# Head mix ahead of the softmax: one float32 matmul becomes three float32r matmuls of split operands

## The chip, the cores and the metric

The kernel runs on one core of one Trainium2 chip. The metric is the device time of one execution in microseconds, given as the median of several runs of the same program. The core's engines are TensorE (PE; its weight loads are shown as PEld), VectorE (DVE), ScalarE (ACT), GpSimd (POOL) and SyncE (SP), which issues nearly all DMA transfers. Each engine works through its own instructions in the order in which the program gives them; semaphores make one engine wait for another.

## The reference, cut to what matters

```python
# batch 2, 12 heads, 448 rows, head size 64
scores = scale * np.matmul(q, k.transpose(0, 1, 3, 2))
scores = np.einsum('bhij,hg->bgij', scores, w_pre)      # head mix ahead of the softmax
scores = scores - np.max(scores, axis=-1, keepdims=True)
attn = np.exp(scores)
attn = attn / (np.sum(attn, axis=-1, keepdims=True) + 1e-09)
attn = np.einsum('bhij,hg->bgij', attn, w_post)         # head mix behind it
attn_out = np.matmul(attn, v)
# rows (b, i) of 12 * 64 values go through two feed-forward layers, 768 -> 2048 -> 768 each
```

All inputs and outputs are float32. The change concerns the first `einsum`.

## The kernel before, in words

**Tiles, groups, steps.** The 448 query rows of each of the two batches are cut into four tiles of 120, 120, 120 and 88 rows. A tile is cut into groups of 10 rows, 12 groups for a tile of 120 and 9 for the tile of 88, so that there are NG = 90 groups. A group holds 10 rows times 12 heads = 120 partitions (GP), with the 448 keys along the free dimension. A loop over steps `s_` runs from -PL to NG + LAG, and in step s the work of several groups is in flight.

**One group's way.** For every head of a tile, `qk` (L193) computes 448 columns of scores in two float32r matmuls, and ScalarE copies them from PSUM into the tile's score buffer S (L600). `pull` (L205) lets SP issue a DMA that gathers one group's rows from S into a buffer "pull" of 120 x 448. `premix` (L221) multiplies the group by the block-diagonal `wpre` (120 x 120), one float32 matmul of 448 columns (L225, two records on TensorE), and VectorE takes the negated maximum of each row (L227). `exp` (L230) is ScalarE's exponential with the row sum as a by-product. `norm` (L213) adds 1e-9 to the sum, inverts it and scales the post-mix weights by it, three VectorE instructions (L216, L217, L219). `post` (L240) is the second mix, eight float32 matmul records per group, LAG = 3 steps behind the first; ScalarE copies its result (L258). When a tile is complete, `av` (L273) multiplies by v, six head pairs per tile.

**Order of the work.** In step s: pull of group s + PL, loads, premix of s, scores of one or two heads of the next tile, exponential of s, copies of these scores, query and key splits, normalisation of s - 1, second mix of s - 3, and whatever the table `also` or `av_at` holds for the step. This order is written out by hand; each engine follows it for its own instructions. The two PSUM buffers "mx" let the mix of group s + 2 start once the exponential of s has read its own.

**Lead times.** PL = 4 steps lie between a pull and its mix, and six buffers "pull" exist. Queries are loaded by SP six steps ahead and split by GpSimd (`split_q`, L165: a rounded copy and a subtraction) two steps ahead. The keys of the second batch are split head by head (`split_k`, L150: a VectorE cast and a GpSimd subtraction) while the last tile of the first batch gets its scores. The v loads of the first batch are issued in steps 0 to 3. `av_at` places three pairs two steps after the second mix of a tile ends, and three pairs half a tile later.

**Towards the feed-forward layers.** Three weight blocks are converted early, in steps that are counted from the third tile from the end (`conv_magnitude` on ScalarE, `conv_shift` and `conv_sign` on VectorE, `conv_round` on GpSimd). From step X on, which is PL steps before the last tile, no scores are left; ScalarE and GpSimd split the attention's results there (`split_x`, L440: a cast on ScalarE, L442, and a subtraction on GpSimd), and `conv_hi` and `conv_lo` split the converted weights. The layers' own matmuls (L447) are three float32r matmuls of split operands: high by high, high by low, low by high.

Of the kernel before, what the change touches and what calls it, by code (L numbers as in the profile page):

```python
# [7 lines left out]
F32 = mybir.dt.float32  # L8
R = mybir.dt.float32r
# [4 lines left out]
ALU = mybir.AluOpType  # L14
# [1 line left out]
PSUM = bass.MemoryType.PSUM  # L16

LAG = 3
PL = 4
EB = 384  # L20

W_MIN = 2.0 ** -15
# [13 lines left out]
def kernel(  # L36
# [15 lines left out]
    nc = tc.nc  # L52
    _, D, H, S = k.shape
# [6 lines left out]
    GP = G * H  # L60
# [3 lines left out]
    tiles = []  # L64
    groups = []
    for b in range(B):
        for i0 in range(0, S, GP):
            n = min(GP, S - i0)
            t = len(tiles)
# [7 lines left out]
    NTILE, NG = len(tiles), len(groups)  # L77
# [23 lines left out]
    with tc.manual_schedule():  # L101
# [30 lines left out]
        def load_v(b, c):  # L132
            t = late.tile([JP, HC, NJ, D], F32, tag=f"v{c}", bufs=1, name=f"v{c}")
            nc.sync.dma_start(out=t, in_=v[b, :, HC * c:HC * (c + 1)])
            v_t[b, c] = t
# [68 lines left out]

        def pull(g):  # L205
            ti, o, st, xn = groups[g]
            t = late.tile([GP, S], F32, tag="pull", bufs=PL + 2, name="pull")
            src = S_t[ti][bass.ds(o, xn, step=st)] if st > 1 else S_t[ti][o:o + xn]
            nc.sync.dma_start(t[:xn * H], src)  # L209
            d_t[g] = t  # L210


        def norm(g):  # L213
# [4 lines left out]
            wr = wr_t[g] = late.tile([GP, GP], F32, tag="wr", bufs=LAG + 1, name="wr")  # L218
            nc.vector.tensor_scalar(wr[:pm], wpost[:pm], sm, None, ALU.mult)  # L219

        def premix(g):  # L221
            pn = groups[g][3] * H
            d = d_t.pop(g)
            m = psA.tile([GP, 512], F32, tag="mx", bufs=2, name="mx")
            nc.tensor.matmul(m[:pn, :S], wpre[:pn, :pn], d[:pn], start=True, stop=True)  # L225
            nm = late.tile([GP, 1], F32, tag="nm", name="nm")
            nc.vector.tensor_reduce(nm[:pn], m[:pn, :S], axis=AX.X, op=ALU.max, negate=True)  # L227
            mx_t[g] = (m, nm)
# [79 lines left out]
        }  # L308
        for ti in range(NTILE - 1):
            lo = tiles[ti]["s"] + tiles[ti]["ng"] + LAG  # L310
            for z in range(2):
                av_at[lo + 2 + z * (tiles[ti + 1]["ng"] // 2)] = [(ti, 3 * z + a) for a in range(3)]


        P = {}
# [56 lines left out]
        def conv_hi(i):  # L372
            if i < len(blocks):
                hi = P["w"].tile([128, WC], R, tag="whi", bufs=3, name="whi")
                nc.scalar.copy(hi, b_t[i])  # L375
                w_t[i] = [hi]

        def conv_lo(i):
            if i < len(blocks):
                lo = P["w"].tile([128, WC], R, tag="wlo", bufs=3, name="wlo")  # L380
                nc.gpsimd.tensor_tensor(lo, b_t.pop(i), w_t[i][0].bitcast(F32), ALU.subtract)  # L381
                m = KD if blocks[i][0] == "in" else 2
                w_t[i] = [x.rearrange("p (k f) -> p k f", k=m) for x in (w_t[i][0], lo)]
# [56 lines left out]
        def split_x(kk, c, a, z, src, eng):  # L440
            h, l = x_pair(kk, c)
            nc.scalar.copy(h[:, a:z], src)  # L442
            eng.tensor_tensor(l[:, a:z], src, h[:, a:z].bitcast(F32), ALU.subtract)
# [82 lines left out]
            nc.sync.dma_start(out=wmix[nm], in_=src)  # L526
        load_q(1, 0)
        wpre = wmix["pre"]

        wpost = late.tile([GP, GP], F32, tag="wpost", bufs=1, name="wpost")  # L530
        for j in range(H // 2):
# [6 lines left out]
        nc.gpsimd.tensor_copy(  # L538
            wpost.rearrange("p (g x) -> p x g", g=H), wmix["post"].rearrange("p (x g) -> p x g", g=H)
        )  # L540
        for s_ in range(-PL, 6 - PL):
            for (ti, h) in qk_at.get(s_, []):
                if h % HC == 0 and h:
                    load_q(ti, h // HC)

        X = tiles[-1]["s"] - PL
        also = {}

        def at(s_, *fs):
            also.setdefault(s_, []).extend(fs)  # L550

        a = tiles[-3]["s"]
        for i in range(NC):
            at(a, lambda i=i: load_w(i))
            for z, f in enumerate((conv_magnitude, conv_shift, conv_sign, conv_round)):
                at(a + 3 + z, lambda f=f, i=i: f(i))
            a += 7
        at(X, open_early)
        at(X + 1, lambda: nc.sync.dma_start(out=alpha_sb, in_=alpha.rearrange("(k p) -> p k", p=128)))
        for kk in range(KD):  # L560
            at(X + 1 + kk, lambda kk=kk: split_x(kk, 0, 0, S, xT[:, kk, :S], nc.gpsimd))
        for i in range(NC):
            at(X + 2 + 3 * i, lambda i=i: conv_hi(i), lambda i=i: conv_lo(i))
        at(X + 7, lambda: load_w(3), lambda: load_w(4))
        at(NG, lambda: conv_a(3))
        at(NG + 1, lambda: conv_round(3))
# [5 lines left out]

        gs = {}
        for s_ in range(-PL, NG + LAG):
            for g in range(PL) if s_ == -PL else [s_ + PL] if 0 <= s_ < NG - PL else []:
                pull(g)
            for c in range(2) if s_ in k_first else ():
                load_k(k_first[s_], c)
            for ti in range(tps, NTILE, tps):
                if s_ == tiles[ti]["s"] + tiles[ti]["ng"] + LAG:  # L580
                    for c in range(4):
                        load_v(tiles[ti]["b"], c)
            if 0 <= s_ < 4:
                load_v(0, s_)
            if s_ in range(NG):
                premix(s_)
            kk = s_ - (NG - KD)
            if kk == 0:
                p0 = ptile()[:, :S]
            if 0 <= kk < KD:  # L590
                in_part(p0, 0, x_t, 0, kk, kk + 1)
            heads = qk_at.get(s_, [])
            pend = [
                qk0(ti, h) if s_ < 0 and h >= HC else qk(ti, h, s_ < 0 and h % 2)
                for (ti, h) in heads
            ]
            if s_ in range(NG):
                exp(s_)
            for d, p in pend:
                nc.scalar.copy(d, p)  # L600
            for (ti, h) in qk_at.get(s_ + 6, []):
                if h % HC == 0:
                    load_q(ti, h // HC)
            for (ti, h) in qk_at.get(s_ + 2, []):
                if h % HC == 0:
                    split_q(ti, h // HC)
            for (ti, h) in qk_at.get(s_ - 2, []):
                if ti % tps == tps - 1 and ti + 1 < NTILE:
                    split_k(tiles[ti + 1]["b"], h)
                    if h in (2, 5):  # L610
                        load_k(tiles[ti + 1]["b"], h // HC + 2)
            if s_ - 1 in range(NG):
                norm(s_ - 1)
            if s_ - LAG in range(NG):
                post(s_ - LAG)
                post_evac(s_ - LAG)
            if s_ == NG:
                p1 = in_chain(1, x_t, 0)
                gs[0, 0] = g_tile(0, 0)
                run(act1(p0, gs[0, 0], 0))  # L620
            if s_ == NG + 1:
                p2 = ptile()[:, :S]
                in_part(p2, 2, x_t, 0, 0, KD // 2)
            if s_ == NG + 2:
                in_part(p2, 2, x_t, 0, KD // 2, KD)
                gs[1, 0] = g_tile(1, 0)
                run(act1(p1, gs[1, 0], 1))
            for (ti, h) in av_at.get(s_, []):
                av(ti, h)
            for f in also.get(s_, []):  # L630
                f()
# [146 lines left out]
```

## Time and profile before

| | us |
|---|---|
| median of three runs | 704.34 |
| lowest and highest | 703.92 and 704.57 |
| the profiled execution, its own time | 703.76 |
| its span, first to last instruction | 701.9 |

| engine | busy us | share of the span | instructions |
|---|---|---|---|
| PE | 692.3 | 99% | 4164 |
| PEld | 608.9 | 87% | 4164 |
| DVE | 440.6 | 63% | 778 |
| ACT | 372.9 | 53% | 692 |
| POOL | 322.6 | 46% | 222 |

A matmul is pipelined, and its end is modelled, so that a busy PE is not yet PE at its peak; how far apart the starts of matmuls lie tells more than the duration listed for one. The chain that ended last is followed back from the last instruction, at each step to what released it or to the instruction before it on its engine. In the table of stretches the engines stand in the order PE, PEld, DVE, ACT, POOL, then come the granted clock (1.00 is full), the busy share of the DMA engines and GB/s. In a row of the timeline the bracket at the end holds the idle time of the engine just before the instruction and what ended it. The attention fills about the first 250 us, the two layers the rest.

### The profile page before, as it was taken

The numbers are of one execution on the slowest core, as the hardware profiler recorded it, in microseconds if no ns is written. First come the engines' busy times: TensorE is split into PE (matmuls) and PEld (weight loads), VectorE is DVE, ScalarE is ACT, GpSimd is POOL, SyncE is SP. The second block draws the span as 40 slices with busy tenths as digits, with TensorE's granted clock in tenths as the row PEclk, the third lists the DMA queues.
The fourth block names the chain that finished last, engine by engine and source line by source line (L and its number), as shares of the span: only waits on it lengthen the run. The fifth ranks groups of instructions, "written<-read, shape, count | busy, mean of one in ns | idle before, by whom it ended". The sixth has DMA issues, their size and how long they took to land.

```text
span 701.9 us, 11158 instructions
## 1 busy us (share of the span) xinstructions
PE 692.3 (99%) x4164; PEld 608.9 (87%) x4164; DVE 440.6 (63%) x778; ACT 372.9 (53%) x692; POOL 322.6 (46%) x222
## 2 busy tenths in 40 slices
PE   7999999999999999999999999999999999999998
PEld 3678778877787999999999999999999999999997
DVE  5565865456666458888874454358999999435311
ACT  5686566667776556656554443343444454445300
POOL 6231552112225335554567555544455455775630
PEclk9999999999999999999999999999999999999999
DMA  4855554346445022423334323322223323445302
GB/s 154 239 175 169 170 138 113 109 161 199 149 99 157 2 90 91 136 90 117 109 115 153 134 93 114 112 91 90 91 91 119 107 91 94 154 156 179 125 1 78
DMA packets 31874, 85.20 MB, mean 121 GB/s; under 512 B 5966, under 2 KB 21966, under 8 KB 31822
## 3 DMA queue, kind: packets, MB, share of 16 engines
q1 hardware_dynamic: 31678, 84.28, 37.2%
q8 instruction: 33, 0.54, 0.3%
q10 hardware_dynamic: 144, 0.23, 0.1%
q14 instruction: 19, 0.16, 0.1%
HBM read 62.47 MB, written 2.75 MB: 93 GB/s over the span
## 4 chain that ended last, share of the span: by engine, by line
PE 88%; POOL 4%; issue 3%; DMA 3%; ACT 1%; SPq 0%; DVE 0%; POOLq 0%; ACTq 0%
PE p L447 58%; PE pt L245 10%; PE mx L225 9%; PE av L282 6%; PE sc L198 4%; POOL wb L370 2%; DMA pull<-S 2%; POOL wlo L381 2%; PE sc L187 1%; DMA qst<-in_q_dram 1%; SPq L209 0%; ACT S L533 0%; ACT S L600 0%; POOL qT L170 0%; DVE o L697 0%
## 5 line engine op out<-in xcount | busy, mean ns | idle before, releaser
L381 POOL TENSOR_TENSOR wlo<-wb,whi 128x768 fp32r<-128x768 f32 x64 | 126.8, 1982 | 126.8 <-ACT whi L375 126.8
L370 POOL TENSOR_TENSOR wb<-wb,wst 128x768 int32<-128x768 int32 x64 | 125.6, 1962 | 102.1 <-DVE wb L363 78.1
L447 PE MATMUL p<-xh,whi 128*128 128x448 f32 x384 | 141.7, 369 | 0.0
L447 PE MATMUL p<-gl,whi 128*128 128x448 f32 x384 | 139.4, 363 | 0.0
L447 PE MATMUL p<-xl,whi 128*128 128x448 f32 x384 | 139.4, 363 | 0.0
L447 PE MATMUL p<-gh,whi 128*128 128x448 f32 x384 | 139.1, 362 | 0.0
L447 PE MATMUL p<-gh,wlo 128*128 128x448 f32 x384 | 138.4, 360 | 0.1
L447 PE MATMUL p<-xh,wlo 128*128 128x448 f32 x384 | 138.3, 360 | 0.0
L355 DVE TENSOR_SCALAR wb<-wb 128x768 f32<-128x768 f32 x64 | 53.1, 829 | 81.2 <-ACT wb L347 81.1
L347 ACT ACTIVATE wb<-wst 128x768 f32<-128x768 f32 x64 | 57.8, 904 | 68.9 <-DMA wst<-in_w_out_dram 48.1
L245 PEld LDWEIGHTS pt<-wr,e 120*112 120x112 f32 x720 | 86.8, 176 | 7.6 <-issue 2.3
L235 ACT ACTIVATE e<-mx,nm 120x448 f32<-120x448 f32 (+1 forms) x90 | 57.4, 638 | 59.9 <-DVE sm L216 46.8
L245 PE MATMUL pt<-wr,e 120*112 120x120 f32 x720 | 88.6, 266 | 0.0
L225 PE MATMUL mx<-pull,wmix_pre 120*120 120x448 f32 x180 | 84.0, 549 | 1.4 <-ACT e L235 1.0
L227 DVE TENSOR_REDUCE nm<-mx 120x1 f32<-120x448 f32 (+1 forms) x90 | 56.0, 622 | 44.4 <-PE mx L225 44.1
L375 ACT CAST whi<-wb 128x768 fp32r<-128x768 f32 x64 | 53.3, 832 | 50.6 <-PE p L447 32.4
L447 PEld LDWEIGHTS p<-xh,whi 128*128 128x128 f32 x384 | 72.1, 188 | 6.7 <-issue 1.2
L447 PEld LDWEIGHTS p<-gh,whi 128*128 128x128 f32 x384 | 72.1, 188 | 5.5
L447 PEld LDWEIGHTS p<-gh,wlo 128*128 128x128 f32 x384 | 71.8, 187 | 5.5 <-POOL wlo L381 0.5
L447 PEld LDWEIGHTS p<-xl,whi 128*128 128x128 f32 x384 | 72.1, 188 | 4.9 <-issue 0.9
L447 PEld LDWEIGHTS p<-xh,wlo 128*128 128x128 f32 x384 | 71.8, 187 | 5.0
L447 PEld LDWEIGHTS p<-gl,whi 128*128 128x128 f32 x384 | 72.1, 188 | 3.9
(52 smaller groups left out, 898.0 us busy)
## 6 DMA issues: line engine op xcount, KB each, us to landing
wst<-in_w_in_dram SPq DMA_DIRECT2D x32, 768.0 KB
wst<-in_w_out_dram SPq DMA_DIRECT2D x32, 768.0 KB
pull<-S SPq DMA_DIRECT2D x88, 210.0 KB
qst<-in_q_dram SPq DMA_DIRECT2D x20, 180.0 KB
kst<-in_k_dram SPq DMA_DIRECT2D x5, 672.0 KB
v<-in_v_dram SPq DMA_DIRECT2D x8, 336.0 KB
out_dram<-o SPq DMA_DIRECT2D x12, 224.0 KB
qst<-in_q_dram SPq DMA_DIRECT2D x8, 132.0 KB
```

The lines of the kernel that those rows point to most:

```text
L198: nc.tensor.matmul(p[:n, :S], t[:, o, a:a + n], kT[h], start=(o == 0), stop=(o == 1))
L225: nc.tensor.matmul(m[:pn, :S], wpre[:pn, :pn], d[:pn], start=True, stop=True)
L227: nc.vector.tensor_reduce(nm[:pn], m[:pn, :S], axis=AX.X, op=ALU.max, negate=True)
L235: nc.scalar.activation(out=e[:pn], in_=m[:pn, :S], func=ACTF.Exp, bias=nm[:pn], accum_out=sm[:pn])
L245: nc.tensor.matmul(p[:, c * GP:(c + 1) * GP], e[:pn, c * JP:(c + 1) * JP], wr[:pn], start=True, stop=True,)
L282: nc.tensor.matmul(p[64 * o:64 * o + 64, a % 3, :n], v_t[T["b"], h // HC][:, h % HC, c, :], MT[ti][:, c, h, :n], start=(c == 0), stop=(c = ...
L347: nc.scalar.activation(t, s[:, :, 1].bitcast(F32), ACTF.Abs)
L355: nc.vector.tensor_scalar(t, t, W_MAX, W_MIN, ALU.min, ALU.max)
L370: nc.gpsimd.tensor_tensor(n, n, st_t.pop(i)[:, :, 0].bitcast(I32), ALU.add)
L375: nc.scalar.copy(hi, b_t[i])
L381: nc.gpsimd.tensor_tensor(lo, b_t.pop(i), w_t[i][0].bitcast(F32), ALU.subtract)
L447: nc.tensor.matmul(p, wt[a], xt[c], start=(first and z == 0), stop=(last and z == 2))
```

## The change

For groups from RAW = 2 on, the mix ahead of the softmax is computed like the layers' matmuls: `wpre` is split once by GpSimd into a rounded high part and the rest, each group's pulled rows are split two steps ahead of their mix into a rounded copy `sh` and the rest (written back over the pulled rows by VectorE), and `premix` issues high by high, high by low, low by high as three float32r matmuls. The copy is ScalarE's for groups in `by_scalar` (two of three, with a few exchanged near the weight conversions) and VectorE's for the others. Groups 0 and 1 keep the float32 matmul. With it go: PL from 4 to 5 with still six pull buffers, queries loaded seven and split three steps ahead, `norm` moved in front of the split, the scores and the query and key splits of its step, all six pairs of `av` in one step, the v loads of the first batch in steps 9 to 12 and those of the second spread over four steps, and other steps for `split_x`, `conv_hi` and `conv_lo`.

```diff
@@ -16,7 +16,8 @@
 PSUM = bass.MemoryType.PSUM
 
 LAG = 3
-PL = 4
+PL = 5
+RAW = 2
 EB = 384
 
 W_MIN = 2.0 ** -15
@@ -204,7 +205,7 @@
 
         def pull(g):
             ti, o, st, xn = groups[g]
-            t = late.tile([GP, S], F32, tag="pull", bufs=PL + 2, name="pull")
+            t = late.tile([GP, S], F32, tag="pull", bufs=PL + 1, name="pull")
             src = S_t[ti][bass.ds(o, xn, step=st)] if st > 1 else S_t[ti][o:o + xn]
             nc.sync.dma_start(t[:xn * H], src)
             d_t[g] = t
@@ -218,11 +219,27 @@
             wr = wr_t[g] = late.tile([GP, GP], F32, tag="wr", bufs=LAG + 1, name="wr")
             nc.vector.tensor_scalar(wr[:pm], wpost[:pm], sm, None, ALU.mult)
 
+        def split_s(g):
+            if RAW <= g < NG:
+                pn = groups[g][3] * H
+                d = d_t.pop(g)
+                t = late.tile([GP, S], R, tag="sh", bufs=2, name="sh")
+                (nc.scalar.copy if g in by_scalar else nc.vector.tensor_copy)(t[:pn], d[:pn])
+                r = d.bitcast(R)
+                nc.vector.tensor_tensor(r[:pn], d[:pn], t[:pn].bitcast(F32), ALU.subtract)
+                d_t[g] = (t, r)
+
         def premix(g):
             pn = groups[g][3] * H
             d = d_t.pop(g)
             m = psA.tile([GP, 512], F32, tag="mx", bufs=2, name="mx")
-            nc.tensor.matmul(m[:pn, :S], wpre[:pn, :pn], d[:pn], start=True, stop=True)
+            if g < RAW:
+                nc.tensor.matmul(m[:pn, :S], wpre[:pn, :pn], d[:pn], start=True, stop=True)
+            else:
+                for z, (a, x) in enumerate(((0, 0), (0, 1), (1, 0))):
+                    nc.tensor.matmul(
+                        m[:pn, :S], wpre_r[a][:pn, :pn], d[x][:pn], start=(z == 0), stop=(z == 2)
+                    )
             nm = late.tile([GP, 1], F32, tag="nm", name="nm")
             nc.vector.tensor_reduce(nm[:pn], m[:pn, :S], axis=AX.X, op=ALU.max, negate=True)
             mx_t[g] = (m, nm)
@@ -308,8 +325,7 @@
         }
         for ti in range(NTILE - 1):
             lo = tiles[ti]["s"] + tiles[ti]["ng"] + LAG
-            for z in range(2):
-                av_at[lo + 2 + z * (tiles[ti + 1]["ng"] // 2)] = [(ti, 3 * z + a) for a in range(3)]
+            av_at[lo + 2] = [(ti, a) for a in range(H // 2)]
 
 
         P = {}
@@ -526,6 +542,7 @@
             nc.sync.dma_start(out=wmix[nm], in_=src)
         load_q(1, 0)
         wpre = wmix["pre"]
+        wpre_r = [late.tile([GP, GP], R, tag=f"wpre{z}", bufs=1, name=f"wpre{z}") for z in "hl"]
 
         wpost = late.tile([GP, GP], F32, tag="wpost", bufs=1, name="wpost")
         for j in range(H // 2):
@@ -538,13 +555,16 @@
         nc.gpsimd.tensor_copy(
             wpost.rearrange("p (g x) -> p x g", g=H), wmix["post"].rearrange("p (x g) -> p x g", g=H)
         )
-        for s_ in range(-PL, 6 - PL):
+        nc.gpsimd.tensor_scalar(wpre_r[0], wpre, 1.0, 1.0, ALU.mult, ALU.mult)
+        nc.gpsimd.tensor_tensor(wpre_r[1], wpre, wpre_r[0].bitcast(F32), ALU.subtract)
+        for s_ in range(-PL, 7 - PL):
             for (ti, h) in qk_at.get(s_, []):
                 if h % HC == 0 and h:
                     load_q(ti, h // HC)
 
         X = tiles[-1]["s"] - PL
         also = {}
+        by_scalar = {g for g in range(NG) if g % 3}
 
         def at(s_, *fs):
             also.setdefault(s_, []).extend(fs)
@@ -554,13 +574,15 @@
             at(a, lambda i=i: load_w(i))
             for z, f in enumerate((conv_magnitude, conv_shift, conv_sign, conv_round)):
                 at(a + 3 + z, lambda f=f, i=i: f(i))
+            by_scalar -= {a + 5}
+            by_scalar |= {a + 7}
             a += 7
         at(X, open_early)
         at(X + 1, lambda: nc.sync.dma_start(out=alpha_sb, in_=alpha.rearrange("(k p) -> p k", p=128)))
         for kk in range(KD):
-            at(X + 1 + kk, lambda kk=kk: split_x(kk, 0, 0, S, xT[:, kk, :S], nc.gpsimd))
+            at(X + 1 + kk + (kk > 1), lambda kk=kk: split_x(kk, 0, 0, S, xT[:, kk, :S], nc.gpsimd))
         for i in range(NC):
-            at(X + 2 + 3 * i, lambda i=i: conv_hi(i), lambda i=i: conv_lo(i))
+            at(X + (3, 8, 10)[i], lambda i=i: conv_hi(i), lambda i=i: conv_lo(i))
         at(X + 7, lambda: load_w(3), lambda: load_w(4))
         at(NG, lambda: conv_a(3))
         at(NG + 1, lambda: conv_round(3))
@@ -572,18 +594,23 @@
 
         gs = {}
         for s_ in range(-PL, NG + LAG):
-            for g in range(PL) if s_ == -PL else [s_ + PL] if 0 <= s_ < NG - PL else []:
-                pull(g)
+            for g in range(2) if s_ == -PL else [s_ + PL + 1] if s_ < -1 else [s_ + PL]:
+                if s_ != -1 and g < NG:
+                    pull(g)
             for c in range(2) if s_ in k_first else ():
                 load_k(k_first[s_], c)
             for ti in range(tps, NTILE, tps):
-                if s_ == tiles[ti]["s"] + tiles[ti]["ng"] + LAG:
-                    for c in range(4):
+                if tiles[ti]["s"] + LAG + 4 <= s_ < tiles[ti]["s"] + LAG + 8:
+                    for c in (s_ - tiles[ti]["s"] - LAG - 4,):
                         load_v(tiles[ti]["b"], c)
-            if 0 <= s_ < 4:
-                load_v(0, s_)
+            if 9 <= s_ < 13:
+                load_v(0, s_ - 9)
             if s_ in range(NG):
                 premix(s_)
+            if s_ - 1 in range(NG):
+                norm(s_ - 1)
+            if s_ in range(NG):
+                split_s(s_ + 2)
             kk = s_ - (NG - KD)
             if kk == 0:
                 p0 = ptile()[:, :S]
@@ -598,10 +625,10 @@
                 exp(s_)
             for d, p in pend:
                 nc.scalar.copy(d, p)
-            for (ti, h) in qk_at.get(s_ + 6, []):
+            for (ti, h) in qk_at.get(s_ + 7, []):
                 if h % HC == 0:
                     load_q(ti, h // HC)
-            for (ti, h) in qk_at.get(s_ + 2, []):
+            for (ti, h) in qk_at.get(s_ + 3, []):
                 if h % HC == 0:
                     split_q(ti, h // HC)
             for (ti, h) in qk_at.get(s_ - 2, []):
@@ -609,8 +636,6 @@
                     split_k(tiles[ti + 1]["b"], h)
                     if h in (2, 5):
                         load_k(tiles[ti + 1]["b"], h // HC + 2)
-            if s_ - 1 in range(NG):
-                norm(s_ - 1)
             if s_ - LAG in range(NG):
                 post(s_ - LAG)
                 post_evac(s_ - LAG)
```

## Rows read from the trace of the kernel before

**Rows 1.** The page's chain that ended last, shares by engine, then by line.

```profile
PE 88%; POOL 4%; issue 3%; DMA 3%; ACT 1%; SPq 0%; DVE 0%; POOLq 0%; ACTq 0%
PE p L447 58%; PE pt L245 10%; PE mx L225 9%; PE av L282 6%; PE sc L198 4%; POOL wb L370 2%; DMA pull<-S 2%; POOL wlo L381 2%; PE sc L187 1%; DMA qst<-in_q_dram 1%; SPq L209 0%; ACT S L533 0%; ACT S L600 0%; POOL qT L170 0%; DVE o L697 0%
```

**Rows 2.** Three stretches: length, busy us of five engines, clock, DMA, GB/s.

```profile
17.80:31.20 13.40, 11.65 (x57) 7.64 (x57) 7.54 (x25) 8.87 (x23) 3.75 (x6) 1.00 0.87 242
...
65.00:85.00 20.00, 20.00 (x186) 16.17 (x186) 17.26 (x41) 13.05 (x33) 12.09 (x13) 1.00 0.49 152
...
200.00:232.00 32.00, 32.00 (x262) 25.76 (x261) 22.47 (x63) 23.75 (x59) 16.09 (x13) 1.00 0.46 110
```

**Rows 3.** The chain of waits in order of time: start us, us, what.

```profile
23.64 7.43 DMA pull<-S
...
33.42 0.75 PE mx L225 x2
...
34.59 0.82 PE pt L245 x8
...
35.41 0.75 PE mx L225 x2
...
82.77 2.61 PE av L282 x48
...
85.62 6.54 DMA pull<-S
...
247.87 298.82 PE p L447 x1493
```

**Rows 4.** VectorE in the timeline: start us, us, engine, line, operation, out<-in.

```profile
110.83 0.62 DVE L227 TENSOR_REDUCE nm<-mx 120x1 f32<-120x448 f32 x1 [0.78 <-PE mx L225]
...
111.75 0.28 DVE L219 TENSOR_SCALAR wr<-wpost,sm 120x120 f32<-120x120 f32 x1
...
205.73 0.28 DVE L219 TENSOR_SCALAR wr<-wpost,sm 120x120 f32<-120x120 f32 x1
...
205.93 0.62 DVE L227 TENSOR_REDUCE nm<-mx 120x1 f32<-120x448 f32 x1
```

**Rows 5.** ScalarE in the timeline, two places.

```profile
80.02 0.57 ACT L258 COPY MT<-pt 112x480 f32<-112x480 f32 x1
...
81.13 0.52 ACT L600 COPY S<-sc 88x448 f32<-88x448 f32 x1
...
81.54 0.57 ACT L258 COPY MT<-pt 112x480 f32<-112x480 f32 x1
...
217.36 0.58 ACT L442 CAST xh<-xT 128x448 fp32r<-128x448 f32 x1
...
217.82 0.66 ACT L235 ACTIVATE e<-mx,nm 120x448 f32<-120x448 f32 x1
```

**Rows 6.** Two lines of VectorE: count, shortest/median/longest ns, first to last start.

```profile
L489 DVE TENSOR_TENSOR gl<-t,gh x32: 611/620/1917, 473.6 to 592.6; 128x448 fp32r<-128x448 f32 x32
...
L219 DVE TENSOR_SCALAR wr<-wpost,sm x90: 277/283/1604, 20.8 to 232.0; 120x120 f32<-120x120 f32 x88, 96x120 f32<-96x120 f32 x2
```

**Rows 7.** VectorE and GpSimd in the timeline of a step that splits keys.

```profile
74.43 0.38 DVE L153 CAST kT<-kst 128x448 fp32r<-128x448 f32 x1
...
74.94 1.14 POOL L154 TENSOR_TENSOR kT<-kst,kT 64x448 fp32r<-64x448 f32 x1 [1.05 <-PE pt L245]
...
75.10 1.06 DVE L219 TENSOR_SCALAR wr<-wpost,sm 120x120 f32<-120x120 f32 x1
```

**Rows 8.** GpSimd in the timeline, the subtraction of a query split.

```profile
102.48 0.95 POOL L170 TENSOR_TENSOR qT<-qst,qT 128x360 fp32r<-128x360 f32 x1
```

**Rows 9.** A weight conversion in the timeline, on ScalarE and VectorE.

```profile
162.68 0.93 ACT L347 ACTIVATE wb<-wst 128x768 f32<-128x768 f32 x1
...
163.64 0.56 DVE L355 TENSOR_SCALAR wb<-wb 128x768 f32<-128x768 f32 x1
...
168.72 0.95 DVE L363 SCALAR_TENSOR_TENSOR wb<-wst,wb 128x768 uint32<-128x768 uint32 x1
```

## The prediction

> **What bounds the kernel now.** I read the chain of waits by line first [rows 1]: 88% of the span is TensorE. 58% is the two feed-forward layers (L447), which the change does not touch; 9% is the head mix ahead of the softmax (L225), 10% the one behind it (L245). The stretches come second [rows 2]: from 65 to 85 us and from 200 to 232 us TensorE is busy without a gap at clock 1.00. Only the first stretch of the attention has holes, 13.40 - 11.65 = 1.75 us. So a microsecond taken from TensorE there is a microsecond of time, until another engine becomes the bound. The chain in order of time gives the step [rows 3]: a mix of 0.75 us at 33.42, one head's scores (from 33.42 + 0.75 = 34.17 to 34.59, 0.42), the second mix of 0.82, next mix at 35.41: 1.99 us. There are 90 such steps.
>
> Third I ask how full the others are in that step. VectorE: from the maximum (110.83) to the scaled weights (111.75) is 0.92 us, and the next instruction follows the scaled weights 0.20 later [rows 4], so 1.12 of 1.99 us. An instruction's listed 0.28 overlaps its successor by 0.08, which I take off listed durations below. ScalarE: from one copy of the second mix (80.02) to the next (81.54), in a place where it never waits, is 1.52 us [rows 5].
>
> **The change, part by part.**
>
> *The matmuls.* 88 of 90 groups get three float32r matmuls of 448 columns for one float32 matmul of 0.75 us. The nearest rows: 1493 float32r matmuls of 448 columns take 298.82 us, 0.200 each, and a head's two take 0.42, 0.21 each [rows 3]. Three are 0.60 to 0.63, the gain 0.12 to 0.15, over 88 groups 10.6 to 13.2 us. The long row has 128 weight columns and is the more exact; I take 0.608, a gain of 0.142 and 12.5 us. The step becomes 1.85 us.
>
> *The split, which nothing hides by itself.* Each of 88 groups adds a copy and a subtraction of 120x448. The subtraction is always VectorE's: the nearest row is a 128x448 subtraction of 0.62 median [rows 6], so 0.54. The copy is VectorE's in one group of three: a 128x448 cast takes 0.38 [rows 7], so 0.30. VectorE's step becomes 1.12 + 0.54 + 0.10 = 1.76 us. ScalarE has the copy in two of three: a 128x448 cast at 217.36 holds it 0.46 [rows 5], so 1.52 + 0.31 = 1.83 us. Against TensorE's 1.85 both have almost no air. The six pair matmuls (5.2 us, two blocks of 2.61 [rows 3], now back to back once per tile) are the only place where they catch up, and only what stands queued: the next maximum needs the next mix, behind the block on TensorE. How far they may fall behind before TensorE feels it: a mix needs its split from two steps before, so 2 x 1.85 = 3.7 us from one mix to the end of the split; 0.9 until the maximum starts, 1.12 and 0.84 of VectorE leave some 0.8.
>
> What is given back I price by stretch.
>
> (a) *Steps with nothing else*, some 44. GpSimd splits queries there, 0.95 us for the subtraction every third step [rows 8]. VectorE's scaled weights take 0.28 alone and up to 1.60 [rows 6]; beside a GpSimd subtraction of 1.14 they took 1.06 [rows 7]. So two-sided: no wait, or 0.95 in three steps, 0.32 a step, giving 1.76 to 2.08 us. Half of it, 0.16, gives 1.92, 0.07 over TensorE: 44 x 0.07 = 3.1 us, of which four pair blocks take back 0.4 each. I take +1.5 (0 to +8).
>
> (b) *The 12 steps that split the second batch's keys.* VectorE adds a cast, 0.30. Before, GpSimd's 1.14 began while the scaled weights came next, and cost them 0.8 [rows 7]. Now the three small instructions are ahead of the cast; the 1.14 runs beside the next maximum and its two successors (0.92), and 0.22 is left. 1.76 + 0.30 + 0.22 = 2.28 against 1.85: 12 x 0.43 = 5.2, less the queue that it starts with and a pair block (some 2): +3 (0, if the wait vanishes and the block covers the rest, to +9, if the old 0.8 stays).
>
> (c) *Three weight conversions in the steps before the last tile.* Each puts two instructions on ScalarE, the first of 0.93, and 0.56, its like and 0.95 on VectorE [rows 9]. In the old step both had 0.5 to 0.9 us of air and TensorE did not stop. Now 2.0 us of VectorE meet 0.09 of air a step, but the change moves a copy off ScalarE in one step and off VectorE in another, and 0.8 may wait. +0.5 each, +1.5 (0 to +5).
>
> (d) *Seven steps without scores* before the feed-forward layers take over. TensorE would need 0.61 + 0.82 = 1.43 a step, and the pair block that stood among them is moved ahead. ScalarE has 1.52 less a score copy (0.41, from 81.13 to 81.54) plus 0.31 plus a cast of the attention's result (0.46) = 1.88 us [rows 5], and a weight cast more: 7 x 0.45 + 0.8 = 3.9. The last splits fall away, so +3.5 (0 to +6).
>
> (e) *The start.* Four loads of v leave the first steps. The pull that the chain waits for landed 7.43 us after its issue [rows 3]; 1.75 us of TensorE stood idle. But the first splits want their rows two steps sooner. -0.5 (-1.7 to +2).
>
> *Costed at nothing:* the two instructions that split the mix weights (GpSimd, once, two steps ahead of use; below a microsecond if they were late, by the 0.95 of a larger one [rows 8]); queries loaded and split a step sooner; the pull five steps ahead with the same six buffers. A pull still needs the buffer of the mix six groups back, so it is issued no sooner in fact than before, while its reader, the split, is two steps sooner. On SP each pull stands behind the wait for that buffer, and query, key and weight loads behind the pull. What hides this is a lead of three steps, 5.5 us; if it doesn't, that is the third rival.
>
> **Sum:** -12.5 + 1.5 + 3 + 1.5 + 3.5 - 0.5 = -3.5 us. The profiled execution took 703.76 us, its span 701.9 with 1.9 around it; that gives 700.3 for such an execution. The median of the three runs is 704.34, 0.6 above it, and 704.34 - 3.5 = 700.8.
>
> **A rule of the Trainium skill.** The rows show the wait: 0.28 us alone, 1.06 beside GpSimd's 1.14 [rows 6, 7]. The Trainium skill, page "SBUF — State Buffer", section "SBUF: two separate sides", says that VectorE and GpSimd share one port pair as an exclusive lock, which an instruction with two SBUF inputs needs as well, and that the loser waits for the whole instruction. This speaks against the change, since the subtraction is of that kind. The trace agrees as far as the 32 subtractions of 0.62 median reach 1.917 us beside GpSimd. By that rule each subtraction is exposed, and the second rival below is what it would lead to.
>
> **Rivals.** *TensorE stays the bound.* For it: waits on GpSimd fall where VectorE waits for ScalarE's copy anyway, and 5.2 us blocks let both engines catch up. Against: 1.83 and 1.76 on average against 1.85, with bursts. It gives -12.5 plus half of (d), 1.8, so -10.7: 694.
>
> *VectorE becomes the bound (the other side).* Place: the subtraction, from the first to the last tile. Price: with the full 0.32 its step is 2.08, 0.09 more than the old 1.99; in (b), (c) and (d) the upper values are half reached, +11 in place of +8. -12.5 + 8 + 11 - 0.5 = +6, or 4 with the pair blocks: 708. It decides from the point where the mean wait passes 0.23 us a step (1.76 + 0.23 = 1.99). For it: VectorE 17.26 of 20 us busy already in (b) [rows 2]. Against: there is one query split in three steps, and the median of the scaled weights is 0.283 [rows 6].
>
> *Pulls land late.* A split that waits holds the exponential queued behind it on ScalarE, or the maximum behind it on VectorE, and TensorE two steps on. Landings of 7.43 and 6.54 us stand in the chain [rows 3], 1 to 2 us more than 5.5; at seven tile changes that is 7 to 14 us, less what the catching up hides, half: +5 on -3.5, 706. Against: the first stands in a stretch that moves 242 GB/s [rows 2], from which four loads are taken; elsewhere TensorE stood still for no pull.
>
> *It doesn't do what it says*: three matmuls of three weight loads run at 0.25 each, and nothing is won. Against: 0.200 with a new weight each time. VectorE's 1.92 then lies below 1.99, and (b) to (d) cost some 5: 709.
>
> **How the numbers follow.** Forecast 0.46 (own range 697.5 to 703.5), TensorE bound 0.17, VectorE bound 0.22, late pulls 0.09, no gain 0.06. What a measurement can tell from no change is 0.2%, 1.4 us. Faster: 0.46 x 0.85 + 0.17 + 0.01 = 0.57. Same: 0.46 x 0.12 and a quarter of the other three, 0.15. Slower 0.28. The range goes from 692.5, near the full gain, to 708, where VectorE bounds.
>
> **What would show it.** Right: three matmuls of a mix 0.20 apart; steps of 1.85 to 1.95 us between pair blocks; TensorE with gaps in (b) and (d) that end with VectorE's or ScalarE's instructions; subtractions of 0.62 mostly, some over 1.2 beside GpSimd. Wrong: steps at 1.85 throughout, or idle TensorE that ends with a pull; a mix still at 0.75.

## The result, and the profile after

The changed kernel takes 710.40 us (median of 5 runs, 707.54 to 710.73), the kernel before beside it 704.26 (5 runs, 703.28 to 704.57): a ratio of 1.0085, 95% interval 1.0066 to 1.0105. It is 6.1 us slower. The forecast was 700.8 with a range to 708; the other side came true, and by more than the rival named for it. The profiled execution has a span of 708.9 us, 7.0 more than before.

The feed-forward layers did not change. In the chain in order of time, their long piece starts at 254.91 in place of 247.87 and lasts the same 298.82 us [rows 3], so the 7.0 us are all ahead of it. Five pieces in order of time (start us, us, what):

```profile
108.82 0.61 PE mx L240 x3
109.43 0.41 PE sc L199 x2
109.84 0.82 PE pt L262 x8
110.67 0.61 PE mx L240 x3
...
254.91 298.82 PE p L463 x1493
```

A mix takes 0.61 in place of 0.75, 0.20 for each of its three matmuls, and a step where nothing waits takes 110.67 - 108.82 = 1.85 us against 1.99. The matmul term stood as forecast there. But of the 89 steps from one second mix to the next only 45 take 1.8 to 1.9 us; in the kernel with the same matmuls and no split (mm_only below) 63 do. The shares of the whole chain, by engine and by line (L240 is now the mix, L229 the subtraction, L244 the maximum):

```profile
PE 74%; DVE 11%; issue 5%; POOL 4%; ACT 2%; DMA 2%; SPq 0%; POOLq 0%; ACTq 0%; DVEq 0%
PE p L463 58%; PE av L299 5%; PE pt L262 5%; PE mx L240 4%; DVE pull L229 4%; DVE nm L244 2%; POOL wb L386 2%; PE sc L199 2%; POOL wlo L397 2%; DMA pull<-S 2%; DVE wr L220 1%; ACT e L252 1%; DVE sm L218 1%; DMA kst<-in_k_dram 1%; DVE kT L154 1%
```

VectorE stood at 0% of it before [rows 1] and has 11% now. The three stretches of rows 2, and in between one of steady steps (length, then busy us and count of TensorE, its weight loads, VectorE, ScalarE and GpSimd; clock, DMA share, GB/s):

```profile
17.80:31.20 13.40, 10.15 (x55) 7.68 (x56) 11.18 (x29) 9.26 (x22) 6.33 (x9) 1.00 0.60 201
65.00:85.00 20.00, 18.49 (x128) 15.13 (x128) 19.34 (x51) 15.61 (x40) 11.89 (x13) 1.00 0.48 147
108.00:116.00 8.00, 8.00 (x60) 7.53 (x59) 7.24 (x22) 7.69 (x20) 0.91 (x3) 1.00 0.45 98
...
200.00:232.00 32.00, 28.11 (x259) 24.52 (x256) 28.07 (x65) 24.45 (x56) 13.51 (x10) 1.00 0.44 110
```

TensorE, which had no gap in the second and last of these, now has 1.5 and 3.9 us of gaps, while VectorE went from 17.26 to 19.34 of 20 us and from 22.47 to 28.07 of 32. Of these four only the steady stretch has TensorE full, with VectorE at 91% and ScalarE at 96%. One step of the second stretch in VectorE's timeline, to be held against the key split of rows 7 (start us, us, engine, line, operation, out<-in):

```profile
73.00 0.14 DVE L217 TENSOR_SCALAR sm<-sm 120x1 f32<-120x1 f32 x1
73.17 0.17 DVE L218 RECIPROCAL sm<-sm 120x1 f32<-120x1 f32 x1
73.37 0.54 DVE L220 TENSOR_SCALAR wr<-wpost,sm 120x120 f32<-120x120 f32 x1
73.83 0.61 DVE L229 TENSOR_TENSOR pull<-pull,sh 120x448 fp32r<-120x448 f32 x1
74.37 0.38 DVE L154 CAST kT<-kst 128x448 fp32r<-128x448 f32 x1
74.67 0.61 DVE L244 TENSOR_REDUCE nm<-mx 120x1 f32<-120x448 f32 x1
75.21 0.14 DVE L217 TENSOR_SCALAR sm<-sm 120x1 f32<-120x1 f32 x1
```

There is no idle time on VectorE, and the step is 75.21 - 73.00 = 2.21 us. The maximum at 74.67 is that of the mix whose last weights were loaded at 72.39, some 2 us before: VectorE is behind. What TensorE waits for in this step is the operand of the second of the three matmuls (high by low): its weight loads stood idle ahead of the subtracted rows,

```profile
72.29 0.18 PEld L240 LDWEIGHTS mx<-pull,wpreh 120*120 120x120 f32 x1 [0.45 <-DVE pull L229]
...
72.39 0.18 PEld L240 LDWEIGHTS mx<-sh,wprel 120*120 120x120 f32 x1
...
74.50 0.18 PEld L240 LDWEIGHTS mx<-pull,wpreh 120*120 120x120 f32 x1 [0.38 <-DVE pull L229]
```

because the subtraction, two steps ahead in the program, is late with everything else on VectorE.

### The profile page after: what moved, and what is told of

Same layout as the page of the kernel before. It is cut to its first block, busy times and chain, and to the rows that moved or that the text cites. A ratio compares the mean times of both kernels' runs of the same rounds, so it can differ in the third digit from the quotient of the medians.

```text
span 708.9 us, 11414 instructions
## 1 busy us (share of the span) xinstructions
PE 685.6 (97%) x4252; PEld 624.5 (88%) x4252; DVE 501.4 (71%) x896; ACT 397.9 (56%) x750; POOL 328.4 (46%) x224
## 4 chain that ended last, share of the span: by engine, by line
PE 74%; DVE 11%; issue 5%; POOL 4%; ACT 2%; DMA 2%; SPq 0%; POOLq 0%; ACTq 0%; DVEq 0%
PE p L463 58%; PE av L299 5%; PE pt L262 5%; PE mx L240 4%; DVE pull L229 4%; DVE nm L244 2%; POOL wb L386 2%; PE sc L199 2%; POOL wlo L397 2%; DMA pull<-S 2%; DVE wr L220 1%; ACT e L252 1%; DVE sm L218 1%; DMA kst<-in_k_dram 1%; DVE kT L154 1%
## 5 line engine op out<-in xcount | busy, mean ns | idle before, releaser
L463 PE MATMUL p<-xh,whi 128*128 128x448 f32 x384 | 139.7, 364 | 0.0
L379 DVE SCALAR_TENSOR_TENSOR wb<-wst,wb 128x768 uint32<-128x768 uint32 x64 | 67.9, 1062 | 1.1
L229 DVE TENSOR_TENSOR pull<-pull,sh 120x448 fp32r<-120x448 f32 (+1 forms) x88 | 61.2, 696 | 3.0 <-ACT sh L227 1.9
```

What stands on the lines that cost most here:

```text
L229: nc.vector.tensor_tensor(r[:pn], d[:pn], t[:pn].bitcast(F32), ALU.subtract)
L379: nc.vector.scalar_tensor_tensor(u, st_t[i][:, :, 1], 0xC0000000, u, ALU.bitwise_and, ALU.bitwise_or)
L463: nc.tensor.matmul(p, wt[a], xt[c], start=(first and z == 0), stop=(last and z == 2))
```

## The experiments

Theory V: the matmul gain is real, and VectorE (then ScalarE) becomes the bound through the time that the split adds. Its rivals: the moved order loses the time (O), or the wait between VectorE and GpSimd does (P). The first four expectations call V theory A, and O theory B.

**First four: one part at a time.** The new order, lead and query split with all mixes in float32; the float32r matmuls without any split (a split of nothing); the copy without the subtraction; and the split in the old order.

```diff
order_only   -RAW = 2
             +RAW = 90
mm_only      -                (copy and subtraction of split_s)
             +                d_t[g] = (d_t[g], d_t[g])     # S and pull tiles float32r
no_sub       -                r = d.bitcast(R)
             -                nc.vector.tensor_tensor(r[:pn], d[:pn], t[:pn].bitcast(F32), ALU.subtract)
             -                d_t[g] = (t, r)
             +                d_t[g] = (t, t)
split_only   -PL = 5
             +PL = 4
             -            av_at[lo + 2] = [(ti, a) for a in range(H // 2)]
             +            for z in range(2):
             +                av_at[lo + 2 + z * (tiles[ti + 1]["ng"] // 2)] = [(ti, 3 * z + a) for a in range(3)]
             ...              (loads, query split, conversions and norm at their old places too)
```

> The changed kernel with the float32 mix kept in all 90 groups and no row split: only the moved order is left (pull and query leads, normalisation ahead, six head pairs in one block, v loads later). Theory A, VectorE and ScalarE become the bound through the added copy and subtraction: the order costs nothing by itself, 703 to 705.5 us. Theory B, it is the moved order (the pair block missing from the end, loads, a shorter lead) that loses the time: 708 to 712 us.

> The changed kernel with the scores rounded to float32r when ScalarE writes them, and the mix reading the pulled rows for both the high and the low operand: three float32r matmuls, no copy, no subtraction (the low part of the rows is left out). Theory A: TensorE stays the bound, 704.3 - 12.5 = 691.8, between 690 and 694 us. Theory B: the order keeps its price, 698 us or more. If a float32r mix were no faster: 704 us.

> The changed kernel without the subtraction: the copies stay (two of three on ScalarE), the mix reads the rounded copy for both operands (the low part of the rows is left out). Theory A with VectorE as the engine that binds: 692 to 696 us, within 3 us of the kernel without copies. Theory A' with ScalarE, whose copy stands ahead of the exponential, as the engine that binds: 700 us or more.

> The kernel before with nothing but the row split two steps ahead and the three matmuls: pulls four steps ahead, the old leads, normalisation at the end of the step, three pairs at a time. Theory A: the same engines bind, and the split of the second batch's keys again costs the scaled weights a wait, 709 to 714 us. Theory B: without the moved order the matmuls pay, 697 to 703 us.

Measured beside the kernel before at 703.76 us (13 runs):

```
order_only  701.51 us, ratio 0.9968 (0.9958 to 0.9978)
mm_only     690.84 us, ratio 0.9822 (0.9808 to 0.9837)
no_sub      694.83 us, ratio 0.9874 (0.9859 to 0.9889)
split_only  718.25 us, ratio 1.0203 (1.0186 to 1.0220)
```

Theory O falls: the order alone gains 2.3 us, and under the split it is worth 718.25 - 710.40 = 7.9. Both runs that show this lie outside both of their forecasts, 701.51 below the 703 to 705.5 of A and 718.25 above its 709 to 714: neither theory had given the new order a gain. The matmuls gain 701.51 - 690.84 = 10.7, or 0.12 in each of 88 groups. The copies give back 4.0, a little more than the 3 forecast, and the subtractions 710.40 - 694.83 = 15.6. So the cost hangs on the subtraction; whether on its time or on its wait, these runs don't tell.

**Time or wait?** First a stand-in of like length with one input, then the subtraction itself with nobody waiting for it.

```diff
sub_as_reduce  -                nc.vector.tensor_tensor(r[:pn], d[:pn], t[:pn].bitcast(F32), ALU.subtract)
               -                d_t[g] = (t, r)
               +                nc.vector.tensor_reduce(x[:pn], t[:pn].bitcast(F32), axis=AX.X, op=ALU.max)
               +                d_t[g] = (t, t)
sub_dead       -                d_t[g] = (t, r)
               +                d_t[g] = (t, t)
```

> The changed kernel with the subtraction of each of the 88 groups replaced by a maximum along the same copied rows (120x448, one input, a result of one column), at the same place in VectorE's order; the mix reads the copy twice, so the low part of the rows is left out. Without the subtraction and without anything in its place the kernel took 694.83 us, with the subtraction 710.40. Theory V (what costs is VectorE's time, some 0.6 us in stretches that are already full): an instruction of like length costs alike, 706 to 711 us if it takes 0.5 to 0.62. Theory P (what costs is the wait of an instruction with two SBUF inputs for GpSimd, and GpSimd's for it): one input does not wait, 695 to 699 us, and no instruction of the stand-in is much longer than its median.

> The changed kernel with every subtraction in its place, but the mix reads the copy twice, so the low part of the rows is computed and left out. No mix waits for a subtraction. The stand-in of like length with one input took 704.0 us, the changed kernel 710.4. Theory P (the 6.4 us between them come from the two SBUF inputs: VectorE's subtraction and GpSimd wait for each other): still there, 709 to 711 us. Theory W (they come from the third matmul, which waits for the subtraction one instruction later than for the copy): gone, 703.5 to 705 us.

The stand-in took 704.02 us (10 runs, 703.09 to 705.62), the unused subtraction 710.34 (4 runs, 709.67 to 712.12); before was at 703.99 and 704.09. The three lines in question (count; shortest, median, longest ns; first and last start; forms), the subtraction of the changed kernel:

```profile
L229 DVE TENSOR_TENSOR pull<-pull,sh x88: 610/624/1557, 20.2 to 238.2; 120x448 fp32r<-120x448 f32 x86, 96x448 fp32r<-96x448 f32 x2
```

the stand-in:

```profile
L229 DVE TENSOR_REDUCE du<-sh x88: 604/616/623, 22.8 to 233.2; 120x1 f32<-120x448 f32 x86, 96x1 f32<-96x448 f32 x2
```

and the unused subtraction:

```profile
L229 DVE TENSOR_TENSOR pull<-pull,sh x88: 610/623/1555, 21.2 to 238.3; 120x448 fp32r<-120x448 f32 x86, 96x448 fp32r<-96x448 f32 x2
```

Medians are alike, and the stand-in has no long one among 88. Grouped by shape (count | busy us, mean ns | idle before, what ended it), the subtractions are busy 58.7 + 2.5 = 61.2 us, the stand-ins 52.9 + 1.2 = 54.1:

```profile
L229 DVE TENSOR_TENSOR pull<-pull,sh 120x448 fp32r<-120x448 f32 x86 | 58.7, 683 | 3.0 <-ACT sh L227 1.9
...
L229 DVE TENSOR_TENSOR pull<-pull,sh 96x448 fp32r<-96x448 f32 x2 | 2.5, 1258 | 0.0
```

```profile
L229 DVE TENSOR_REDUCE du<-sh 120x1 f32<-120x448 f32 x86 | 52.9, 615 | 3.8 <-ACT sh L227 2.8
...
L229 DVE TENSOR_REDUCE du<-sh 96x1 f32<-96x448 f32 x2 | 1.2, 607 | 0.0
```

The stand-in's 704.02 us lies between the two forecasts, outside both (706 to 711 for V, 695 to 699 for P): each was half right, V with the larger half. 704.02 - 694.83 = 9.2 of the 15.6 us come with plain VectorE time. 710.34 - 704.02 = 6.3 come with what the stand-in lacks, the second SBUF input and the 448 written columns. The written columns do not lengthen the instruction by themselves, since the medians are alike. All 13 subtractions above 0.7 us ran beside an instruction of GpSimd that had begun before them, as here:

```profile
98.45 1.19 POOL L155 TENSOR_TENSOR kT<-kst,kT 64x448 fp32r<-64x448 f32 x1
98.57 1.56 DVE L229 TENSOR_TENSOR pull<-pull,sh 120x448 fp32r<-120x448 f32 x1
```

Of the stand-ins 17 began within an instruction of GpSimd, and none was long. The 6.3 us are about the 7.1 by which the subtractions are longer in sum.

That the second matmul needs the subtracted rows adds nothing to the total: 710.34 and 710.40 are the same. The wait is there, 10.5 us of idle weight loads ahead of the subtracted rows in the changed kernel, but without it a longer wait ahead of the first matmul stands in its place. Its share for ScalarE's exponential doubles, from 3.9 to 7.8 us, and nearly all that the exponential itself waits for is VectorE (the changed kernel first, then the unused subtraction):

```profile
L240 PEld LDWEIGHTS mx<-pull,wpreh 120*120 120x120 f32 x86 | 15.8, 184 | 10.5 <-DVE pull L229 10.2
L240 PEld LDWEIGHTS mx<-sh,wpreh 120*120 120x120 f32 x86 | 15.7, 182 | 11.7 <-ACT MT L275 4.1 <-ACT e L252 3.9 <-POOL qT L171 2.1
```

```profile
L240 PEld LDWEIGHTS mx<-sh,wpreh 120*120 120x120 f32 x172 | 25.1, 186 | 16.8 <-ACT e L252 7.8 <-ACT MT L275 4.0 <-POOL qT L171 2.2
...
L252 ACT ACTIVATE e<-mx,nm 120x448 f32<-120x448 f32 x88 | 56.5, 642 | 29.0 <-DVE sm L217 14.2 <-DVE nm L244 13.8
```

The Trainium skill, page "SBUF — State Buffer", section "SBUF: two separate sides", names two SBUF inputs among the things that make VectorE take the port pair that GpSimd needs; one input and two inputs differ here as it says. One input alone is no protection, though: the scaled weights read a single large tensor and took 1.06 us beside GpSimd in place of 0.28 before the change [rows 6, 7].

**Moving work between the engines.** The subtraction to GpSimd; and all copies to ScalarE.

```diff
sub_pool  -                nc.vector.tensor_tensor(r[:pn], ...
          +                nc.gpsimd.tensor_tensor(r[:pn], ...
copy_act  -                (nc.scalar.copy if g in by_scalar else nc.vector.tensor_copy)(t[:pn], d[:pn])
          +                nc.scalar.copy(t[:pn], d[:pn])
```

> The changed kernel with the subtraction of each group on GpSimd in place of VectorE. GpSimd is busy 328 us and gets 88 x about 1.1 = 97 more, far from full on average. Theory V (VectorE's time costs): the 0.62 us leave the full engine, 695 to 700 us. Theory P (the wait between VectorE and GpSimd costs): every step now has an instruction of about 1.1 us on GpSimd, and the scaled weights, 0.28 alone, take up to 1.0 beside it in each step, so nothing is won or more is lost: 708 to 725 us, with a median of the scaled weights well above 0.28.

> The changed kernel with all 88 copies on ScalarE: VectorE loses 30 casts of 0.41 us, 12.4 us in all, half of them in stretches where it is full; ScalarE gets them at some 0.45. Theory V1 (VectorE alone is full): about 6 us are gained, 703 to 706 us. Theory V2 (ScalarE is as full as VectorE there): what one engine wins the other loses, 709 to 713 us.

On GpSimd it took 720.23 us (ratio 1.0223, 1.0205 to 1.0241). The scaled weights have a median of 546 ns there in place of 284, as theory P asked; but TensorE's weight loads waited mostly for GpSimd itself, busy 1.16 us a group beside its other splits:

```profile
L229 POOL TENSOR_TENSOR pull<-pull,sh 120x448 fp32r<-120x448 f32 x86 | 98.9, 1157 | 50.2 <-PE mx L240 19.6 <-ACT sh L227 15.1 <-DVE sm L217 4.5
```

```profile
L220 DVE TENSOR_SCALAR wr<-wpost,sm x90: 279/546/1342, 21.3 to 251.3; 120x120 f32<-120x120 f32 x88, 96x120 f32<-96x120 f32 x2
```

```profile
L240 PEld LDWEIGHTS mx<-pull,wpreh 120*120 120x120 f32 (+1 forms) x88 | 16.3, 186 | 27.5 <-POOL pull L229 27.3
```

So this run falls in the range of theory P by another mechanism, and does not say how much the wait alone costs. With all copies on ScalarE it took 705.31 (ratio 1.0023, 1.0011 to 1.0034), 5.1 us less than the changed kernel: 30 casts off VectorE won them, as theory V1 had it. The Trainium skill, page "Perfetto Trace Analysis", section "Optimizing Scalar/DVE Operations", says that moving work to ScalarE may make sense where VectorE is saturated, and warns that a move between VectorE and GpSimd might not help for the shared port. The 5.1 us agree with the first; the second came out as warned, but what the trace shows there is a late GpSimd, so the port's part stays open.

**Splitting only where VectorE has air**, that is, time in a step in which it would have nothing to do. The mix is split for chosen groups and stays float32 for the others; the order is the new one. In the fourth run the copies from group 36 on move to ScalarE as well.

```diff
-RAW = 2
+SPLIT = {*range(6, 25), *range(46, 58)}                                            # select1, 31 groups
+SPLIT = {*range(6, 25), *range(26, 46, 2), *range(46, 58), *range(58, 72, 2)}      # select2, 48
+SPLIT = {*range(3, 25), *range(45, 59), 88, 89}                                    # select3, 38
+SPLIT = {*range(3, 25), *range(36, 60), 88, 89}                                    # select4, 48; copies of g >= 36 on ScalarE
-            if RAW <= g < NG:
+            if g in SPLIT:
-            if g < RAW:
+            if g not in SPLIT:
```

> The changed kernel, its order kept, with the split and the three float32r matmuls for 31 groups only (6 to 24 and 46 to 57), those of the stretches in which the subtraction was seen to cost nothing; the others keep their float32 mix. Theory V: in these stretches TensorE is the bound and gains about 0.12 a group, 31 x 0.12 = 3.7, and nothing is given back elsewhere: 701.5 (order alone) - 3.7 = 697.8, range 697 to 699. Rival R (what the split costs hangs on the count of splits wherever they stand, 19.6 us / 88 = 0.22 a group): 701.5 - 3.7 + 6.9 = 704.7.

> As with 31 groups, and every second group of 26 to 45 and 58 to 71 on top, 48 groups. Theory V: a split in every second step adds 0.3 to 0.46 us a step to VectorE, half of what filled it; in the steps with air it fits (17 x 0.12 = 2.0 gained), in those that split the second batch's keys (58 to 71) it does not, and some 0.3 us for each of 7 is lost: 696.5 to 699. Rival R: 701.5 - 5.8 + 10.6 = 706.

> As with 31 groups, with 3 to 5, 45, 58, 88 and 89 added, 38 groups. By theory V each added group gains about 0.1 us where VectorE still has air: the first three steps took 5.54 us with the split and 5.82 without, the last four 9.43 and 9.61. 697.84 - 0.28 - 0.18 - 0.1 = 697.3, range 696.3 to 698.3; if 3 to 5 make the start late, up to 699.

> As with 38 groups, and groups 36 to 44 and 59 split as well, 48 groups, with the copies of 36 and above all on ScalarE. With all copies there, the stretch from the 33rd to the 42nd second mix took 22.63 us, with no split 23.51, and the one after it no longer than with a third of them on VectorE. Theory V1 (VectorE's time decides, and ScalarE has air here): 697.87 - 0.8 = 697.1, range 696.2 to 698. Rival (each further split costs as much as its matmuls gain): 697.9 or more.

```
select1  697.84 us, ratio 0.9907 (0.9892 to 0.9921)
select2  699.85 us, ratio 0.9933 (0.9916 to 0.9949)
select3  697.87 us, ratio 0.9915 (0.9901 to 0.9928)
select4  696.72 us, ratio 0.9888 (0.9872 to 0.9904)
```

The first hit its forecast of 697.8 and fells rival R (704.7). The second missed (696.5 to 699): splits in every second group of the full stretches, expected neutral on the whole, lost 2.0 us against the first. The third changed nothing; 697.87 is within its range, but of the 0.5 us that it was to gain nothing is seen. The last, with 48 groups as in the second but chosen by air, is 1.1 us under the third (more groups and moved copies together; no run tells them apart) and the best of the kernels that leave nothing out: 7.5 us under the kernel before and 13.7 under the change. Of the 7.5 the new order by itself makes up 2.3. In it the second and third stretch of rows 2 have TensorE almost full again, and VectorE 4.7 and 10.8 us of air:

```profile
65.00:85.00 20.00, 19.92 (x192) 16.69 (x190) 15.26 (x44) 13.47 (x34) 16.44 (x17) 1.00 0.58 182
200.00:232.00 32.00, 31.20 (x255) 26.05 (x255) 21.17 (x58) 23.75 (x59) 16.05 (x14) 1.00 0.38 97
```

## Why the prediction was wrong

Set against the same kernel without a split (690.84), the split gives back 19.6 us. By place, from the starts of the second mixes in the profiled executions, each against that of mm_only (one execution each; "copies" is no_sub, "stand-in" sub_as_reduce, "unused" sub_dead, "change" the changed kernel):

```
term of the prediction                second mixes  forecast   copies  stand-in  unused  change
(e) the start                         up to the 3rd   -0.5       +0.9     +3.8    +5.2    +1.8
(a) steps with nothing else           3-21, 33-54     +1.5       +0.1     +0.1    +1.1    +1.8
(b) keys of the second batch          21-33           +3.0       +1.0     +3.4    +5.5    +5.6
(c) weight conversions                54-72           +1.5       +1.4     +4.5    +5.1    +7.1
(d) steps without scores              72-88           +3.5       +0.8     +3.1    +3.4    +3.8
sum of what is given back                             +9.0       +4.2    +15.0   +20.3   +20.1
the matmuls (order_only to mm_only)                  -12.5                              -10.7
the new order by itself               in (e)                                             -2.3
```

The matmul term was right in kind (0.61 in place of 0.75) and 1.8 us too large. The step that failed is the price of the split in stretches that hold other work: (c) above all, forecast at 1.5 and measured at 7.1, then (b), 3 and 5.6, and the start. The numbers of (a) and (d) held, but not for the reasons given. (a) was priced as a wait of the scaled weights for GpSimd; these did not change, and it is the subtraction that waits, since the stand-in loses 0.1 there. (d) was priced as ScalarE's load, 1.88 us a step; with its copies alone the stretch loses 0.8, VectorE's stand-in makes it 3.1, and with all copies on ScalarE (copy_act) it lost no more than the change, 3.6. It also holds the third conversion, which was priced in (c): VectorE's part of it starts at 206.21 us, behind the 72nd second mix at 204.8. That the number of (d) came out is luck.

- (c) I wrote that a moved copy and 0.8 us of queue hide most of a conversion. Each puts about 2 us on VectorE and 1.7 on ScalarE, and a step had some 0.1 of air. VectorE's subtractions lie at 185.80, 188.51 and 192.39, steps of 2.7 and 3.9 us with the conversion's instructions between them, and in the second of them scaled weights of 1.23 us beside the conversion's instruction on GpSimd (0.28 alone). That wait stood in the kernel before as well, and I had not added it to the 2 us:

```profile
185.80 0.62 DVE L229 TENSOR_TENSOR pull<-pull,sh 120x448 fp32r<-120x448 f32 x1 [0.67 <-ACT sh L227]
186.34 0.55 DVE L371 TENSOR_SCALAR wb<-wb 128x768 f32<-128x768 f32 x1
186.93 0.56 DVE L372 TENSOR_SCALAR wb<-wb 128x768 uint32<-128x768 uint32 x1
...
188.51 0.62 DVE L229 TENSOR_TENSOR pull<-pull,sh 120x448 fp32r<-120x448 f32 x1
189.05 0.95 DVE L379 SCALAR_TENSOR_TENSOR wb<-wst,wb 128x768 uint32<-128x768 uint32 x1
...
190.13 1.84 POOL L386 TENSOR_TENSOR wb<-wb,wst 128x768 int32<-128x768 int32 x1 [5.08 <-ACT MT L275]
...
190.83 1.23 DVE L220 TENSOR_SCALAR wr<-wpost,sm 120x120 f32<-120x120 f32 x1
```

  In the copies alone this place (second mixes 66 to 72) already lost 1.4 us, with either the subtraction or its stand-in 3.8: what is lost there does not hang on the second input. A late pull is in the 7.1 as well (a piece of the chain, start and us; in the execution of the unused subtraction the six steps there were 1.8 us shorter):

```profile
151.41 9.22 DMA pull<-S
```

- (b) The step forecast at 2.28 us was measured at 2.21 (above). What failed is the 2 us that I took off for the queue and the pair block: 12 x (2.21 - 1.85) = 4.3 at least, and a step with a copy on VectorE as well is longer; 5.6 were measured.
- (e) is not settled: the first second mix stood at 25.6 us in the changed kernel and 23.8 without a split, but at 25.2 in the run of the order alone, which has no split either. The run of 31 groups, which has the same program as the order alone up to that point, has it at 23.5, so a single execution varies by 1.7 us there, about as much as was to be explained. The start is also in the 9.2 and the 6.3 us: without it the profiled executions give 7.9 for plain time, 3.9 for the second input, and 3.2 more for the changed kernel than for the unused subtraction, 2 of them around the late pull.
- The new order I had priced at nothing but the start. It gains 2.3 us alone and 7.9 under the split. Which of its moves does it, no run tells.

Of the rivals, "VectorE becomes the bound" is what happened, at 710.4 in place of 708. That the numbers are near is partly luck: its +11 for (b) to (d) does not follow from the bounds given, whose upper values add up to 20. Its place was right only in part, since steps with nothing else lost little, and its mechanism half: I let the mean wait of the scaled weights decide. Those did not grow (a median of 284 ns, before 283 [rows 6]); what decides is VectorE's own 0.62 a group, 9.2 us, with 6.3 for the waits of the subtraction itself. Late pulls happened once. "Three matmuls win nothing" fell at the first pair of rows.

What misled me in the working: I compared mean loads of a step (1.76 and 1.83 against 1.85) and found that both fit. In plain steps they do: there the stand-in costs 0.1 us over 39 steps. But I priced each extra burst against queues and the catching up of pair blocks. With 0.02 to 0.09 of air a step little is caught up: in (b) the 12 steps lost 5.6 us, where the excess of each over 1.85 adds up to 4.3 at least.

## What to carry to other kernels

Where work is moved from a full engine to one which is at 90% or more, the receiving engine's load is to be added up stretch by stretch, with the bursts and waits that already stand there, and what exceeds the step counted as time, without credit for catching up. A trade of this kind need not be made everywhere: made only where the receiving engine has air, and with some copies moved to ScalarE, the split turned +6.1 us into -7.5; without what the new order gives by itself, 7.5 - 2.3 = 5.2 gained. And an instruction's cost can be told from its wait by a stand-in of like length with other operands, its reader's wait by keeping it and leaving its result unused, if one also looks at what the reader waits for then.

## What was not expected of the hardware

A reduction of 120x448 from one SBUF input never took over 623 ns, 17 of 88 begun beside GpSimd's instructions, while a subtraction of the same size with two took up to 1557 (9 of 88 over 1 us in the changed kernel), and the kernels differ by 6.3 us. The same subtraction takes 1157 ns on GpSimd and 683 on VectorE on average, waits included.
